# Attention, gated layer and hard-swish layer on one core: the seven-product blocks' matmuls taken in alternation with those of the neighbouring products

## The chip, the core and the metric

The kernel runs on one core of a Trainium2 chip. The metric is the device time of one execution in microseconds, the median of several. The engines are TensorE (PE, with its weight loads PEld), VectorE (DVE), ScalarE (ACT), GpSimd (POOL, which here mostly issues DMAs) and SyncE (SP, which issues the loads from memory). Each engine takes its instructions in the order in which the program has them.

## The reference

Three layers follow each other. `x` of the second is the first's output, 896 tokens of 768 numbers.

```python
attn = softmax(causal(scale * q @ k.T)); x = attn @ v             # 2 x 12 heads, 448 tokens, 64 wide
gate = 1.0 / (1.0 + np.exp(-(x @ w_gate))); val = x @ w_val       # 768 -> 1536, twice
x = (gate * val) @ w_out                                          # 1536 -> 768
h = x @ w_in; g = h * np.clip(h + 3.0, 0.0, 6.0) / 6.0            # 768 -> 2048
out = g @ w_out2                                                  # 2048 -> 768
```

## The kernel before

**Numbers.** The weights come as 64-bit words. Each unit of 128 x 768 is loaded by SP and made into float32 by five steps (`dec_scale` on ACT, line 115; `dec_shift`, `dec_clamp`, `dec_join`, `dec_sign` on DVE, lines 120, 124, 128, 134). Every operand of a matmul is then split into a rounded part `hi` and a rest `lo`, and every product of two operands is three matmuls (`TERMS`: hi with hi, hi with lo, lo with hi). A split is done in one of two ways. `split` (lines 181 and 182) and `dec_hi`/`dec_lo` (153 and 158) copy on ACT and subtract on DVE. `dma_split` (142 to 144) copies and negates on ACT and lets a DMA issued by POOL add the source onto the negative: in the rows that DMA is `lo<-S` or `lo<-raw`.

**Stages.** Attention goes first. The gate and value layer follows with eight plain units (`halves`, line 190) and then the FIRST run of seven-product blocks. `halves` again makes the 1536 -> 768 product and then four plain units of the 2048-wide layer. The THIRD run of seven-product blocks does the rest of that layer, and `block` (line 1203) the last product. In `halves` each set of weights is used twice in a row, for two halves of the tokens, which go to two PSUM banks: its matmuls alternate between banks already. `block` and the seven-product blocks keep to one bank for a whole product.

**Seven-product blocks.** `Pairs.run` takes two weight units at a time (a pair p; eight pairs in FIRST, six in THIRD). The four quarters of the two units and of the activations are combined by sums (`w_sums`, DVE lines 727 to 730), so that seven half-sized products P1 to P7 do the work of eight. A product (`product`, line 750) is nine matmuls of 128 x 448: three chunks of the inner dimension times three terms. A pair has three PSUM banks. Bank 0 collects P1, then P6, then P7, then P4; what stands there between two of them is copied out by ACT (`copy_out`, line 767) before the next may add to it. Bank 1 collects P5 and then P3 and is added by DVE (`add_out`, line 771); bank 2 holds P2. The order on PE is P1(p), P2(p), P4(p-1), P6(p), P3(p-1), P5(p), P7(p); after the last pair come its P4 and P3. The weights of a product are named by their group: group 1 for P1 and P2 (`g`), group 2 for P6 and P5 (`hi`, `lo`), group 3 for P7 and P3 (`hi`, `lo`), group 4 for P4 (`g`). Groups 2 and 3 of the next pair are made by `dma_split` from the sums, one pair ahead. `finish` and `p4_out` apply the gate (`glu`, ACT line 919 and DVE line 917) or the hard swish (`hardswish`, ACT 1087 and DVE 1088), and `end1`, `end2`, `end3` start the splits that the next stage needs.

Of the kernel before, what the change touches and what calls it, by code (L numbers as in the profile page):

```python
# [21 lines left out]
TERMS = ((0, 0), (0, 1), (1, 0))  # L22
# [9 lines left out]
def kernel(  # L32
# [12 lines left out]
    nc = tc.nc  # L45
# [4 lines left out]
    P = 128  # L50
# [14 lines left out]
    HK = KD // 2  # L65
# [145 lines left out]
    with tc.manual_schedule():  # L211

        with ExitStack() as actx:
# [212 lines left out]
            def product(cols, stationary=P):  # L426

                return max(cols / 2.4 + 3, stationary / 1.2)


            steps = []
            for p in range(NP):
# [11 lines left out]
                for i, ts in enumerate(STILES):  # L444
                    work = sum(
                        6 * product(Q1[t], Q1[t] - Q0[t]) + 2 * product(Q1[t] - Q0[t], 0) for t in ts
                    )
                    add(f"S{i}", "pe", work, ["Tlq", "Tlk"], s_pe, ts)
                    for t in ts:
                        add(f"M{t}", "dve", 70 + 2.1 * Q1[t], [f"S{i}"], s_max, t)  # L450
                for t in range(NQ):
                    n = Q1[t]
# [3 lines left out]
                for g in range(NG):  # L456
                    m = WIDTH[g]
                    tiles = [f"N{t}" for t in range(NQ) if Q1[t] > GROUPS[g][0][0] * D]
                    add(f"C{g}", "pe", 0.87 * m, tiles, c_pe, g)
                    add(f"H{g}", "act", 60 + m / 1.2, [f"C{g}"], c_hi, g)  # L460
                    add(f"J{g}", "dve", 70 + m / 0.96, [f"H{g}"], c_lo, g)
                    work = sum(3 * product(S - c * D) for c, _ in GROUPS[g])
                    add(f"D{g}", "pe", work, [f"J{g}", "Vl", f"D{g - 1}"][: 2 + (g > 0)], d_pe, g)
# [13 lines left out]
            for u in range(3):  # L477
                w = f"{u}"
# [188 lines left out]
        def w_dec():  # L667

            i = stream[0]
            stream[0] += 1  # L670
            u = order[i]
            decode_a(u)
            if i + 3 < NU:
                load_unit(order[i + 3])
            if u not in in_pairs:
                behind.append(u)

        def w_parts():
            while behind:
                u = behind.pop(0)  # L680
                (dec_dma if u < len(order1) else decode_b)(u)

        def tiles_at(i, n):
            return [gact.tile([P, UN], F32R, tag=f"e{i + x}", name="g") for x in range(n)]

        class Pairs:
# [7 lines left out]
            def __init__(self, units, form, s_at, g1_at, g4_at, hold, p4_out, finish, ahead):  # L694
                self.units, self.form, self.hold = units, form, hold
                self.s_at, self.g1_at, self.g4_at = s_at, g1_at, g4_at
                self.P4_out, self.finish, self.ahead = p4_out, finish, ahead
                self.n = len(units)
                self.grp, self.banks = {}, {}

            def w_g1(self, p):
                if p < self.n:
# [40 lines left out]
                self.w_g(p, 3)  # L743

            def product(self, ps, w, off, nm, first):
                x = self.form[nm]
                for i in range(HK):
                    k = off * HK + i
                    for n, (a, c) in enumerate(TERMS):
                        nc.tensor.matmul(  # L750
                            ps,
                            lhsT=w[a][:, k * P : (k + 1) * P],
                            rhs=x[:, c, i],
                            start=(first and i == 0 and n == 0),
                            stop=(i == HK - 1 and n == 2),
                            skip_group_check=True,
                        )

            def P1(self, p):
                self.banks[p] = [  # L760
# [45 lines left out]
            def P3_add(self, p):  # L806
                self.add_out(p, 1, "C12")

            def run(self, end1, end2, end3):

                for p in range(self.n):
                    end = p == self.n - 1
                    self.P1(p)
                    self.P1_out(p)
                    if p:
                        self.P7_add(p - 1)
                    if p or not self.ahead:  # L820
                        self.w_g1(p + 1)
                        w_dec()
                    self.P2(p)
                    self.w_g1_lo(p + 1)
                    self.P2_add(p)
                    if p:
                        self.P4(p - 1)
                        self.P4_out(p - 1)
                    self.P6(p)
                    self.P6_out(p)  # L830
                    if self.ahead and p == 0:
                        y_split("T4")
                    self.w_sums(p + 1)
                    if p:
                        self.P3(p - 1)
                        self.P3_add(p - 1)
                    if end:
                        end1()
                    self.w_g4(p + 1)
                    self.w_g2(p + 1)  # L840
                    self.P5(p)
                    soon = p and self.soon(p - 1)
                    if not end:
                        w_parts()
                    if soon:
                        self.finish(p - 1)
                    if not end:
                        w_dec()
                    if p and not soon:
                        self.finish(p - 1)  # L850
                    self.P7(p)
                    self.P7_out(p)
                    if end:
                        self.P7_add(p)
                        end2()
                    else:
                        self.w_g3(p + 1)
                p = self.n - 1
                self.P4(p)
                self.P4_out(p)  # L860
                self.P3(p)
                w_parts()
                end3()
                self.P3_add(p)
                self.finish(p)
# [64 lines left out]
        def g4_at1(p):  # L930
            return [t[:, :HU] for t in tiles_at(4 * (p % 2) + 2, 2)]

        first = Pairs(
            [(at1[f, v], at1[f + 1, v]) for f, v in pairs1], form1, s1_at,
            lambda p: tiles_at(4 * (p % 2), 2), g4_at1, hold1, p4_out1, finish1, False,
        )
# [127 lines left out]
        def y_split(nm):  # L1064
            form3[nm] = gact.tile([P, 2, HK, S], F32R, tag=f"r{nm}", name=nm)
            h, b = {"T2": (0, 0), "T1": (0, 1), "T4": (HK, 0), "T3": (HK, 1)}[nm]
            for i in range(HK):
                split(
                    form3[nm][:, 0, i], form3[nm][:, 1, i], yr[h + i][:, b * S : (b + 1) * S]
                )  # L1070
# [199 lines left out]
```

## Time and profile before

| | us |
|---|---|
| median of 3 runs (606.36 to 607.29) | 607.05 |
| span of the profiled execution | 604.3 |
| PE busy in it | 591.4 |
| DVE busy | 476.4 |
| ACT busy | 346.1 |
| the chain that ended last, by engine | PE 56%, DVE 27%, ACT 9%, POOL 3%, DMA 2% |

The profile covers one execution from its first to its last instruction; what its own time has beside the span is not recorded, and the median of the runs lies 2.75 us above the span. A matmul's row in the trace lasts about 365 ns and overlaps the next one; the distance between the starts of two matmuls is what one costs. An "idle" in brackets is time in which no row of that engine runs, with the name of what ended it, so a wait is somewhat longer than the idle beside it.

### The profile page before, as it was taken

Reading aid. Unit: us, or ns where it says so; the run is one execution under the profiler, and the core shown is the slowest. Engines: PE = TensorE matmul, PEld = TensorE weight load, DVE = VectorE, ACT = ScalarE, POOL = GpSimd, SP = SyncE. Lnnn points to the kernel's source line nnn. Section 1 sums busy time; section 2 is a strip of 40 time slices with the busy share of each in tenths; the row PEclk is TensorE's granted clock in tenths of the full one; section 3 lists DMA queues with packets and bytes.
Section 4 is the critical chain, followed back from the end, with each engine's and each line's share of the span. In section 5 each row is a group of like instructions: output and inputs, shape, how many; then the busy total and the mean of one; then the engine's idle time right before and its main releaser. Section 6 shows DMA issues by size and latency. Waiting matters only on the chain.

```text
span 604.3 us, 9071 instructions
## 1 busy us (share of the span) xinstructions
PE 591.4 (98%) x3372; PEld 535.8 (89%) x3372; DVE 476.4 (79%) x739; ACT 346.1 (57%) x680; POOL 136.7 (23%) x195
## 2 busy tenths in 40 slices
PE   8999999999999999999999999999999999999997
PEld 4788788899998999998999999988999899999997
DVE  6789998568797898988967787888999888867601
ACT  3898998735656656667443333387677645533200
POOL 4889988401111111110000000012222000000000
PEclk9999999999999999999999999999999999999999
DMA  7665341036985876674334434367988514437002
GB/s 167 137 178 132 81 143 33 0 79 167 263 178 133 215 183 180 166 177 129 82 114 150 154 115 135 94 165 165 235 217 200 140 53 112 131 124 227 23 1 91
DMA packets 86684, 82.64 MB, mean 137 GB/s; under 512 B 35312, under 2 KB 77040, under 8 KB 86640
## 3 DMA queue, kind: packets, MB, share of 16 engines
q1 hardware_dynamic: 80448, 64.50, 35.9%
q0 software_dynamic: 6192, 17.57, 15.8%
q8 instruction: 26, 0.43, 0.3%
q14 instruction: 18, 0.15, 0.1%
HBM read 61.73 MB, written 2.75 MB: 107 GB/s over the span
## 4 chain that ended last, share of the span: by engine, by line
PE 56%; DVE 27%; ACT 9%; POOL 3%; issue 3%; DMA 2%; SPq 0%; ACTq 0%; POOLq 0%; DVEq 0%
PE w L750 25%; PE m L1203 12%; PE m L190 10%; DVE b L128 4%; DVE b L134 4%; DVE lo L158 4%; PE pav L392 3%; ACT hi L153 3%; PE s L309 2%; DVE g L1171 2%; PE pt L365 2%; DVE b L124 2%; DVE raw L120 2%; ACT pr L337 2%; DVE g L182 2%
## 5 line engine op out<-in xcount | busy, mean ns | idle before, releaser
L1203 PE MATMUL m<-hi,g 128*128 128x384 f32 x448 | 114.0, 335 | 0.6 <-DVE g L1171 0.6
L153 ACT CAST hi<-b 128x768 fp32r<-128x768 f32 x35 | 29.0, 835 | 104.3 <-DVE b L134 100.1
L1203 PEld LDWEIGHTS m<-hi,g 128*128 128x128 f32 x448 | 80.8, 188 | 1.2 <-DVE g L1171 1.2
L1203 PE MATMUL m<-lo,g 128*128 128x384 f32 x224 | 74.9, 335 | 0.4 <-DVE lo L158 0.4
L750 PE MATMUL w<-T,hi 128*128 128x448 f32 x252 | 72.4, 368 | 1.4 <-ACT g2r L767 1.4
L190 PE MATMUL m<-g,hi 128*128 128x448 f32 x288 | 70.1, 365 | 0.0
L134 DVE SCALAR_TENSOR_TENSOR b<-raw,b 128x768 int32<-128x768 int32 x68 | 66.0, 971 | 2.3
L128 DVE SCALAR_TENSOR_TENSOR b<-b,raw 128x768 int32<-128x768 int32 x68 | 65.4, 962 | 2.3
L115 ACT ACTIVATE b<-raw 128x768 f32<-128x768 f32 x68 | 61.2, 905 | 0.0
L124 DVE TENSOR_SCALAR b<-b 128x768 f32<-128x768 f32 x68 | 38.1, 561 | 25.5 <-ACT b L115 25.2
L190 PEld LDWEIGHTS m<-g,hi 128*128 128x128 f32 x288 | 54.1, 188 | 4.3
L144 POOL DMA_DIRECT2D lo<-S x26 | 25.2, 971 | 131.0 <-ACT lo L143 102.5
L352 POOL TENSOR_SCALAR pr<-pr,rc 64x64 f32<-64x64 f32 (+3 forms) x96 | 52.6, 565 | 9.1 <-DVE rc L346 7.3
L158 DVE TENSOR_TENSOR lo<-b,hi 128x768 fp32r<-128x768 f32 x35 | 33.3, 957 | 27.0 <-ACT hi L153 26.9
L750 PEld LDWEIGHTS w<-T,hi 128*128 128x128 f32 x252 | 47.2, 188 | 6.3 <-ACT g2r L767 1.8
L190 PE MATMUL m<-x,hi 128*128 128x448 f32 x192 | 49.1, 367 | 0.0
L337 ACT ACTIVATE pr<-s,nm 64x64 f32<-64x64 f32 (+3 forms) x96 | 44.4, 469 | 5.7 <-PE s L319 5.0
L750 PE MATMUL w<-T,lo 128*128 128x448 f32 x126 | 46.5, 369 | 0.7 <-DMA lo<-S 0.5
L1203 PEld LDWEIGHTS m<-lo,g 128*128 128x128 f32 x224 | 42.0, 188 | 0.7 <-DVE lo L158 0.7
L392 PE MATMUL pav<-pth,vpad 128*128 128x448 f32 (+6 forms) x168 | 41.0, 309 | 0.0
L190 PE MATMUL m<-g,lo 128*128 128x448 f32 x144 | 40.9, 366 | 0.0
L190 PEld LDWEIGHTS m<-x,hi 128*128 128x128 f32 x192 | 35.7, 188 | 2.7
(139 smaller groups left out, 1248.8 us busy)
## 6 DMA issues: line engine op xcount, KB each, us to landing
raw<-in_moe_w_out_dram SPq DMA_DIRECT2D x28, 768.0 KB, 4.5
raw<-in_moe_w_in_dram SPq DMA_DIRECT2D x16, 768.0 KB, 4.7
lo<-S POOLq DMA_DIRECT2D x26, 384.0 KB, 4.3
raw<-in_moe_w_gate_dram SPq DMA_DIRECT2D x12, 768.0 KB, 5.2
raw<-in_moe_w_val_dram SPq DMA_DIRECT2D x12, 768.0 KB, 5.0
k<-in_k_dram SPq DMA_DIRECT2D x24, 112.0 KB, 2.7
q<-in_q_dram SPq DMA_DIRECT2D x24, 112.0 KB, 3.0
v<-in_v_dram SPq DMA_DIRECT2D x24, 112.0 KB, 2.9
```

Source lines behind the costliest of these rows:

```text
L115: nc.scalar.activation(b, words(u)[0].bitcast(F32), AF.Copy, scale=REBIAS)
L124: nc.vector.tensor_scalar(b, b, UPPER_MAX, -UPPER_MAX, op0=ALU.min, op1=ALU.max)
L128: nc.vector.scalar_tensor_tensor(bi, bi, 3, words(u)[1], op0=ALU.logical_shift_left, op1=ALU.bitwise_or)
L134: nc.vector.scalar_tensor_tensor(bi, words(u)[0], -(2 ** 31), bi, op0=ALU.bitwise_and, op1=ALU.bitwise_or)
L153: nc.scalar.copy(hi, part_t[u])
L158: nc.vector.tensor_sub(lo, part_t.pop(u), split_t[u][0].bitcast(F32))
L190: nc.tensor.matmul(ps[:, b, :S], lhsT=w[a][:, i * P : (i + 1) * P], rhs=x(c, k0 + i, b), start=(first and i == 0 and n == 0), stop=(last a ...
L337: nc.scalar.activation(pr[:, :, j], ps[:, j].rearrange("p (c d) -> p c d", d=D), AF.Exp, bias=nm[:, j : j + 1], accum_out=sm[:, j : j + 1],)
L352: nc.gpsimd.tensor_scalar(pr[:, :, j], pr[:, :, j], rc[:, j : j + 1], 1.0, op0=ALU.mult, op1=ALU.mult)
L392: nc.tensor.matmul(live["pav", p][:, c * D :], lhsT=vpad[p % NV][a][:, c], rhs=pt[e][:, off : off + S - c * D], start=(c == 0 and m == 0), ...
L750: nc.tensor.matmul(ps, lhsT=w[a][:, k * P : (k + 1) * P], rhs=x[:, c, i], start=(first and i == 0 and n == 0), stop=(i == HK - 1 and n == ...
L1203: nc.tensor.matmul(po[t], lhsT=g2[2 * s + i][a][:, t * P : (t + 1) * P], rhs=w[e][:, i * HC : (i + 1) * HC], start=(s == 0 and i == 0 and ...
```

## The change

`product` no longer emits its nine matmuls in one piece. It emits the first four in alternation with the five that the product before it left over, and leaves its own last five to the next call. `flush` emits what is left where no product follows at once. The readers of a product stand one product later in the program, since a product now ends in its successor's call. In the last pair P3 comes before P4, and what bank 1 holds of P5 is copied out by ACT (`P5_out`) before P3 adds to it, while bank 0 with P7 is added by DVE (`P5_add`) before P4. `P7_out` and `w_g3` move from the end of a pair to the start of the next.

```diff
             def product(self, ps, w, off, nm, first):
                 x = self.form[nm]
-                for i in range(HK):
+                def one(i, n, a, c):
                     k = off * HK + i
-                    for n, (a, c) in enumerate(TERMS):
-                        nc.tensor.matmul(
...
+                steps = [(i, n, a, c) for i in range(HK) for n, (a, c) in enumerate(TERMS)]
+                head = len(steps) // 2
+                for m in range(max(len(self.rest), head)):
+                    if m < len(self.rest):
+                        self.rest[m]()
+                    if m < head:
+                        one(*steps[m])
+                self.rest = [lambda st=st: one(*st) for st in steps[head:]]
+
+            def flush(self):
+                for mm in self.rest:
+                    mm()
+                self.rest = []
...
+            def P5_out(self, p):
+                nc.scalar.copy(self.hold(p, "C22"), self.banks[p][1])
+
+            def P5_add(self, p):
+                self.add_out(p, 0, "C22")
...
                     self.P1(p)
+                    if p:
+                        self.P7_out(p - 1)
+                        self.w_g3(p)
+                    self.P2(p)
                     self.P1_out(p)
                     if p:
                         self.P7_add(p - 1)
                     if p or not self.ahead:
                         self.w_g1(p + 1)
                         w_dec()
-                    self.P2(p)
+                    if p:
+                        self.P4(p - 1)
+                    else:
+                        self.flush()
                     self.w_g1_lo(p + 1)
                     self.P2_add(p)
+                    self.P6(p)
                     if p:
-                        self.P4(p - 1)
                         self.P4_out(p - 1)
-                    self.P6(p)
+                        self.P3(p - 1)
+                    else:
+                        self.flush()
                     self.P6_out(p)
...
+                    self.P5(p)
                     if p:
-                        self.P3(p - 1)
                         self.P3_add(p - 1)
...
-                    self.P5(p)
+                    self.P7(p)
+                    if end:
+                        self.P5_out(p)
...
-                    self.P7(p)
-                    self.P7_out(p)
-                    if end:
-                        self.P7_add(p)
-                        end2()
-                    else:
-                        self.w_g3(p + 1)
                 p = self.n - 1
+                self.P3(p)
+                self.P5_add(p)
+                end2()
                 self.P4(p)
+                self.flush()
                 self.P4_out(p)
-                self.P3(p)
                 w_parts()
                 end3()
                 self.P3_add(p)
```

On PE at the start of the FIRST run, before (`x_70` is P1's operand, `x_72` P2's, `T_2308` P6's, the rows above are the plain units):

```order
L190 MATMUL m<-x_72,lo 128x448
L190 MATMUL m<-x_73,lo 128x448
L750 MATMUL w<-x_70,g 128x448 x9
L750 MATMUL w<-x_72,g 128x448 x9
L750 MATMUL w<-T_2308,hi 128x448 x2
```

and now:

```order
L751 MATMUL w<-x_70,g 128x448 x5
L751 MATMUL w<-x_72,g 128x448
L751 MATMUL w<-x_70,g 128x448
L751 MATMUL w<-x_72,g 128x448
L751 MATMUL w<-x_70,g 128x448
L751 MATMUL w<-x_72,g 128x448
L751 MATMUL w<-x_70,g 128x448
L751 MATMUL w<-x_72,g 128x448
L751 MATMUL w<-x_70,g 128x448
L751 MATMUL w<-x_72,g 128x448 x5
L751 MATMUL w<-T_2308,hi 128x448 x2
```

P1 ended with PE's ninth matmul of the run and now ends with its thirteenth; P6 starts with the nineteenth in both.

On PE at the end of the THIRD run, before (`T_4492` is P7's operand, `T_4594` P4's, `y_3667` P3's; line 1203 is the next stage):

```order
L750 MATMUL w<-T_4492,hi 128x448 x2
L750 MATMUL w<-T_4492,lo 128x448
L750 MATMUL w<-T_4594,g 128x448 x9
L750 MATMUL w<-y_3667,hi 128x448 x2
```

and now:

```order
L751 MATMUL w<-T_4492,hi 128x448
L751 MATMUL w<-y_3667,lo 128x448
L751 MATMUL w<-T_4492,hi 128x448
L751 MATMUL w<-y_3667,hi 128x448
L751 MATMUL w<-T_4492,lo 128x448
L751 MATMUL w<-y_3667,hi 128x448
L751 MATMUL w<-T_4594,g 128x448
L751 MATMUL w<-y_3667,lo 128x448
L751 MATMUL w<-T_4594,g 128x448
L751 MATMUL w<-y_3667,hi 128x448
L751 MATMUL w<-T_4594,g 128x448
```

P4, which stood between P7 and P3, is now the last product, and five of its matmuls follow P3's end.

On ACT in the last pair of the THIRD run, before (`h<-g2r` and `t<-g2r` are `finish` of the pair before, the copy between the two `g` rows is the one of bank 0 after P7):

```order
L767 COPY g2r<-w 128x448
L1170 ACTIVATE g_5191<-g2r 128x896
L1087 ACTIVATE h<-g2r 128x448
L1087 ACTIVATE t<-g2r 128x896
L767 COPY g2r<-w 128x448
L1170 ACTIVATE g_5191<-g2r 128x896
L1087 ACTIVATE h<-w 128x448
L153 CAST hi<-b 128x768 x2
```

and now, with the new copy of bank 1 after P5:

```order
L782 COPY g2r<-w 128x448
L1198 ACTIVATE g_5195<-g2r 128x896
L825 COPY g2r<-w 128x448
L1115 ACTIVATE h<-g2r 128x448
L1115 ACTIVATE t<-g2r 128x896
L1198 ACTIVATE g_5195<-g2r 128x896
L1115 ACTIVATE h<-w 128x448
L153 CAST hi<-b 128x768 x2
```

The copy moved ahead of `finish`; the same happens at the end of FIRST. Apart from this move, ACT, DVE, POOL and SP have the same instructions in the same order as before, in both runs.

## Rows read from the trace of the kernel before

**Rows 1.** The page: span, busy time of the engines, and one line of its DMA issues.

```profile
span 604.3 us, 9071 instructions
...
PE 591.4 (98%) x3372; PEld 535.8 (89%) x3372; DVE 476.4 (79%) x739; ACT 346.1 (57%) x680; POOL 136.7 (23%) x195
...
lo<-S POOLq DMA_DIRECT2D x26, 384.0 KB, 4.3
```

**Rows 2.** Busy time by stretch, FIRST and line 190's: engines, granted clock, DMA.

```profile
179.20:284.30 105.10, 104.30 (x505) 94.45 (x504) 91.62 (x141) 66.29 (x100) 13.32 (x14) 1.00 0.67 173
284.30:401.10 116.80, 116.80 (x577) 108.12 (x577) 94.59 (x131) 51.03 (x71) 2.80 (x4) 1.00 0.41 119
```

**Rows 3.** Timeline, PE in FIRST: start of P1 of pairs 0 to 3.

```profile
179.21 3.81 PE L750 MATMUL w<-x,g 128*128 128x448 f32 x18
...
188.32 3.81 PE L750 MATMUL w<-x,g 128*128 128x448 f32 x18
...
201.67 3.88 PE L750 MATMUL w<-x,g 128*128 128x448 f32 x18
...
214.69 1.61 PE L750 MATMUL w<-x,g 128*128 128x448 f32 x7
```

**Rows 4.** Timeline, start of FIRST: ACT's first copy and split, PE's P6(1).

```profile
181.23 0.53 ACT L767 COPY raw<-w 128x448 f32<-128x448 f32 x1 [4.96 <-PE w L750]
...
188.37 0.83 ACT L142 CAST hi<-raw 128x768 fp32r<-128x768 f32 x1 [1.91 <-DVE raw L728]
...
194.54 0.47 PE L750 MATMUL w<-T,lo 128*128 128x448 f32 x1 [0.18 <-DMA lo<-raw]
```

**Rows 5.** Timeline, group 2's DMA in FIRST and THIRD; the PE row is P6(7)'s.

```profile
201.96 1.20 POOL L144 DMA_DIRECT2D lo<-S  x1 [8.15 <-PE w L750]
...
267.69 0.84 POOL L144 DMA_DIRECT2D lo<-S  x1 [8.29 <-ACT lo L143]
...
272.76 0.37 PE L750 MATMUL w<-T,lo 128*128 128x448 f32 x1
...
426.29 1.20 POOL L144 DMA_DIRECT2D lo<-S  x1 [5.94 <-ACT lo L143]
...
465.35 1.19 POOL L144 DMA_DIRECT2D lo<-S  x1 [5.93 <-ACT lo L143]
```

**Rows 6.** Timeline, end of FIRST: P7's last matmul, P4, DVE, line 190.

```profile
279.58 0.37 PE L750 MATMUL w<-T,lo 128*128 128x448 f32 x1
280.57 2.09 PE L750 MATMUL w<-T,g 128*128 128x448 f32 x9 [0.62 <-ACT h L767]
...
285.14 0.56 PE L190 MATMUL m<-g,lo 128*128 128x448 f32 x2
...
280.55 0.62 DVE L771 TENSOR_TENSOR h<-w,h 128x448 f32<-128x448 f32 x1 [1.66 <-ACT h L767]
...
283.94 1.82 DVE L158 TENSOR_TENSOR lo<-b,hi 128x768 fp32r<-128x768 f32 x2
```

**Rows 7.** Timeline, PE at the start of THIRD: P6(0) and P6(1).

```profile
406.33 0.67 PE L750 MATMUL w<-T,hi 128*128 128x448 f32 x2 [1.39 <-ACT g2r L767]
...
418.46 0.47 PE L750 MATMUL w<-T,lo 128*128 128x448 f32 x1 [0.52 <-DMA lo<-S]
```

**Rows 8.** Timeline, end of THIRD: PE, ACT and DVE.

```profile
478.45 2.09 PE L750 MATMUL w<-T,g 128*128 128x448 f32 x9 [0.62 <-ACT g2r L767]
...
482.89 0.44 PE L1203 MATMUL m<-lo,g 128*128 128x384 f32 x1 [0.35 <-DVE lo L158]
...
475.07 0.95 ACT L1087 ACTIVATE t<-g2r 128x896 f32<-128x896 f32 x1
...
480.58 0.55 ACT L1087 ACTIVATE h<-w 128x448 f32<-128x448 f32 x1 [1.33 <-PE w L750]
...
476.49 1.08 DVE L1088 SCALAR_TENSOR_TENSOR g2r<-t,g2r 128x896 f32<-128x896 f32 x1
...
481.88 1.83 DVE L158 TENSOR_TENSOR lo<-b,hi 128x768 fp32r<-128x768 f32 x2
```

More of the change, by code (lines that the diff above doesn't have):

```diff
@@ L698, in __init__ @@
                 self.n = len(units)
-                self.grp, self.banks = {}, {}
+                self.grp, self.banks, self.rest = {}, {}, []
             def w_g1(self, p):
@@ L746, in product @@
                 x = self.form[nm]
-                for i in range(HK):
+                def one(i, n, a, c):
                     k = off * HK + i
-                    for n, (a, c) in enumerate(TERMS):
-                        nc.tensor.matmul(
[L751 to L757, printed above, removed]
+                    nc.tensor.matmul(
+                        ps,
+                        lhsT=w[a][:, k * P : (k + 1) * P],
+                        rhs=x[:, c, i],
+                        start=(first and i == 0 and n == 0),
+                        stop=(i == HK - 1 and n == 2),
+                        skip_group_check=True,
+                    )
+                steps = [(i, n, a, c) for i in range(HK) for n, (a, c) in enumerate(TERMS)]
[10 more added lines that the diff above has]
+                self.rest = []
             def P1(self, p):
```

## The prediction

> **What bounds the kernel now.** The page comes first: PE is busy 591.4 us of a span of 604.3 [rows 1], so the kernel ends when PE has got through its matmuls, and time can be won only from the pace of a matmul or from PE's few waits. The table by stretch shows the TensorE clock at its upper level (1.00 of 2.4 GHz) in FIRST as in the stage of line 190 [rows 2].
>
> The pace is read from starts. FIRST begins with P1, P2, P6, P5, P7 of pair 0, 45 matmuls, from 179.21 to P1(1) at 188.32: 202.4 ns each. From P1(2) at 201.67 to P1(3) at 214.69 lie 63 in 13.02 us: 206.7 ns [rows 3]. Line 190, which alternates between two banks, makes 577 in 116.80 us, 202.4 ns [rows 2]. So there are two paces 4.3 ns apart, and one bank alone has both; the slower one begins behind P6(1)'s wait for `lo`.
>
> The waits of the two runs stand in three kinds of places. P6(1) waits for the DMA that makes its `lo` [rows 4, 7]. P6(0) of THIRD waits for ACT [rows 7]. In the last pair P4 waits until ACT has copied P7 out of bank 0: 279.58 to 280.57 is 0.99 where 0.20 is usual [rows 6], and THIRD shows the same idle of 0.62 [rows 8]. Line 1203 then waits for its first `lo` [rows 8].
>
> Beside PE runs a chain that it does not pace: sums on DVE, `hi` and the negative on ACT, POOL's DMA, the next decode, `w_g1`, the next sums. Group 2's DMA goes out at 201.96 and five pairs later at 267.69, 13.15 us a pair; in THIRD at 426.29 and three pairs later at 465.35, 13.02 [rows 5]. That is as long as PE's own 13.02, so a faster PE would soon wait for it. Its slack at P6(7): issue 267.69, landing 4.3 later by the page's median [rows 1] = 272.0, use 272.76 [rows 5].
>
> **The change, part by part.** Let a position be one matmul (0.207 us). A product's first four matmuls now stand 4, 3, 2 and 1 positions earlier, its last one 4 later; only the third needs `lo`, 2 positions (0.41) earlier. The number of matmuls stays the same, and no DMA is moved past another.
>
> *In the middle pairs: 0.* A copy-out that waits for PE comes 0.83 later, and bank 0 still has ten positions between two products. No row there shows DVE or the chain of group 2 waiting behind those copies for long. The cover is the chain's slack of about 0.8 against 0.41 asked. Without it each pair would lose up to 0.4.
>
> *(a) Start of FIRST: +1.2.* P1(0) ends 4 positions later (0.81 at 202.4 ns). ACT has been idle 4.96 us for it [rows 4], and behind that copy stand `w_g1`, the decode scale, through it DVE's decode and sums, and ACT's `hi<-raw`, which waited for DVE [rows 4]. All of it comes 0.81 later, and so does the `lo` for which P6(1) waits at 194.54 [rows 4]. This `lo` is now needed two positions earlier in the row, so PE has 0.41 more behind it: 0.81 + 0.41 = 1.22.
>
> *(b) Last pair of FIRST: +0.6.* Before, one wait: 0.99 - 0.20 = 0.79, and one slow step after it (0.1: the row at 194.54 [rows 4], also behind a wait, lasts 0.47 where those of [rows 5, 6] last 0.37), 0.9 in all. Now two. P3's first matmul stands two positions behind P5's last and waits for the copy: 0.99 - 0.41 + 0.1 = 0.68. P4's first stands two behind P7's last and waits for DVE's add, 0.62 [rows 6] where the copy takes 0.53 [rows 4]: 0.77. Together 1.45, so 0.55 more.
>
> *(c) Into line 190: +1.0.* P4 is now last. DVE's multiply of its result (0.62, the form of the add in [rows 6]) and then the first of two subtractions for the next stage's `lo` (1.82 for both [rows 6], 0.91 each) follow P4's end; before, P3's nine matmuls covered them and 285.14 shows no idle [rows 6]. From P4's last start: 0.37 + 0.04 + 0.6 + 0.95 = 1.95; line 190 uses `lo` five positions (1.0) later, so 0.95, and 0.1 after it.
>
> From here to THIRD the same chain of DVE and ACT is late by (a) to (c), and P6(0) of THIRD waits for ACT anyhow, 1.39 idle [rows 7]; nothing is lost again.
>
> *(d) Start of THIRD: +0.4.* The chain there does not hang on P1(0)'s end, since ACT comes late to it. The `lo` at 418.46 [rows 7] comes as before and finds PE two positions further from the end: 0.41.
>
> *(e) Last pair of THIRD: +0.95.* First wait 0.68 as in (b). With (d) P5's last matmul starts at 477.46 (0.99 before P4 [rows 8]) + 0.41 - 5 x 0.207 = 476.83. The copy is done at 476.83 + 0.41 + 0.53 = 477.77, P3 starts at 477.82, P7's last at 477.82 + 0.10 + 7 x 0.2025 = 479.34. Behind that copy on ACT now stand `finish`'s two steps, the second of which was done at 475.07 + 0.95 = 476.0 before [rows 8]; ACT's `t` (0.95) ends at about 479.1, DVE's step with it takes 1.08 [rows 8], and only then comes the add of 0.62: 480.8. P4's first would have been at 479.75, so 1.05 and 0.1 after it. 0.68 + 1.15 - 0.88 = 0.95.
>
> *(f) Into line 1203: +1.8.* Before, P4 ended at 480.54 (ACT starts on it at 480.58 [rows 8]) and line 1203's first `lo` matmul ran at 482.89, behind ACT's relu, ACT's `hi` and DVE's `lo` at 481.88 [rows 8]: 2.35. With P4 last that is 2.35 + 0.37 after its last start, where 0.41 is usual: 2.3 lost, and 0.1. Before, 0.6 was lost there. So 1.8.
>
> *(g) Pace: between 0 and -1.0, taken -0.3.* If the pairs keep the 206.7 ns that followed a wait for `lo` in [rows 3], nothing changes. If they keep 202.4, each pair is 0.27 us shorter until PE meets the chain of 13.15 and 13.02. Banks leave less: P6 now starts four positions earlier behind ACT's copy. I allow 0.55 in FIRST and 0.45 in THIRD. Line 190's alternation speaks for the fast pace, the wait for `lo` that remains against it, so a third of it is taken.
>
> Sum: 1.2 + 0.55 + 1.05 + 0.4 + 0.95 + 1.8 - 0.3 = 5.65. On the span 604.3 that gives about 609.9; with the 2.75 us by which the median of the runs lies above it, 612.7.
>
> The Trainium skill, "TensorE: Matmul & The Clock Gate", section "Back-to-back issue gap", gives an isolated warm gap of N / 2.4 + 2.5 ns whatever the bank, which would be 189 ns for 448 columns. The trace disagrees with 202.4 and 206.7; by the page neither bank nor order would change the pace, and (g) would be 0.
>
> **The rivals.**
> *The ends cost less.* The `lo` subtractions may be got through earlier, or the next stage may make up the delay in slack that I did not see, so that (c) and (f) are nothing: 612.7 - 2.85 = 609.9. For it speaks that line 1203 has only 0.6 of wait there now; against it that DVE and ACT take their instructions in order and both stand behind P4's result.
>
> *Line 190's stage falls to the slow pace* after its new wait: 577 x 4.3 ns = 2.5 us, of which 1.5 vanish in P6(0)'s wait [rows 7]: 613.7, up to 615.2 if that cover is gone. No row shows the slow pace in alternating matmuls.
>
> *Faster: alternating lifts the pace itself* for all 882 matmuls of the blocks (14 pairs of 7 products of 9). Losses of 5.95 are repaid when a matmul costs 6.7 ns less than the mean of about 205.8, that is below 199 ns, and only if the chain of group 2 is not what holds the pairs. At 189 ns (the distance that pure streaming at 2.4 GHz would nearly give, 448 / 2.4 = 187) it would be 613.0 - 882 x 16.8 ns = 598.2. Against it: line 190 alternates and has 202.4 [rows 2], and the chain's 13.15 us a pair is longer than 63 x 202.4 = 12.75. The gap of 189 ns that the Trainium skill gives on the page named above is the same number.
>
> *No change:* the copy of P1(0) or the waits of the last pairs are covered by something that I misread, and the fast pace gives back the rest: 607.
>
> *The clock falls.* At 1.2 GHz 448 columns take 373 ns, and 882 x 167 ns = 147 us. Line 190 alternates at 1.00 [rows 2]. The Trainium skill, "TensorE: Matmul & The Clock Gate", section "A second HAM failure mode: psum-queue depth-cycling", tells of a kernel that lost clock by cycling banks in every iteration; by that rule this change would be dangerous, by the row it is not.
>
> **How the numbers follow.** The forecast, (a) to (g) as summed, 611.8 to 613.3: 0.52. Ends cheaper, 609.3 to 611.8: 0.20. Slower pace in line 190 or a further wait in the middle pairs, 613.3 to 615.5: 0.14. No change, within 0.2% (1.2 us, about what runs of this kernel can tell apart): 0.06. Faster pace: 0.06. Clock: 0.02. The range 609.4 to 614.5 leaves out the last three and the far end of the third case. Faster 0.06, same 0.06, slower 0.88.
>
> **What would show it.** In FIRST P6(1)'s `lo` matmul starts near 195.35, with a longer idle before it. Each last pair shows two idles before PE rows, one ended by ACT's copy, one by DVE's add, the second longer in THIRD. The first `lo` of line 190 shows a wait for DVE's subtraction, that of line 1203 one of about 2 us. Group 2's DMAs stay 13.15 and 13.02 apart. The prediction is wrong if the distance between starts in the pairs drops below 199 ns, if those DMAs draw closer together, or if the ends of the runs show no longer waits.

## The result and the profile after

The changed kernel takes 612.33 us (median of 6 runs, 611.62 to 613.56) against 606.7 of the kernel before (6 runs, 604.41 to 608.58). The ratio is 1.0105, 95% interval 1.0085 to 1.0124: slower by 6.4 us (5.2 to 7.5); the two medians lie 5.6 apart. The forecast was 612.7, from 609.4 to 614.5.

The page of the profiled execution, its first line and the one of busy times [rows 1]:

```profile
span 610.6 us, 9072 instructions
...
PE 595.1 (97%) x3372; PEld 536.1 (88%) x3372; DVE 476.3 (78%) x739; ACT 345.7 (57%) x680; POOL 136.3 (22%) x195
```

The number of matmuls is the same and the span is 6.3 us longer. By stretch (FIRST, line 190's, and 3.2 us at the start of the last product; the columns as in [rows 2]):

```profile
179.10:285.60 106.50, 104.06 (x505) 93.96 (x504) 90.67 (x139) 66.53 (x101) 13.29 (x14) 1.00 0.66 171
285.60:405.66 120.06, 119.30 (x577) 108.03 (x576) 96.57 (x133) 52.54 (x74) 3.50 (x5) 1.00 0.40 117
...
490.40:493.60 3.20, 3.20 (x12) 3.20 (x12) 2.72 (x4) 3.20 (x4) 0.00 (x0) 0.51 0.00 0
```

FIRST is 1.4 us longer than before and line 190's stage 3.3. The third row is a surprise that is taken up at the end: the clock granted there is half.

The start of FIRST, ACT's copy of P1(0) and PE's P6(1), in the timeline [rows 4]:

```profile
181.94 0.54 ACT L782 COPY raw<-w 128x448 f32<-128x448 f32 x1 [5.76 <-PE w L751]
...
195.23 0.47 PE L751 MATMUL w<-T,lo 128*128 128x448 f32 x1 [0.33 <-DMA lo<-raw]
```

FIRST begins at 179.11, 0.10 earlier than before. ACT has been idle 5.76 us where it was 4.96, and `lo` is used 16.12 us behind the start where it was 15.33.

The end of FIRST, PE and then DVE (L825 is the new copy of bank 1, L786 the add, L945 the multiply of P4's result) [rows 6]:

```profile
280.12 0.48 PE L751 MATMUL w<-x,hi 128*128 128x448 f32 x1 [0.42 <-ACT h L825]
...
282.81 0.47 PE L751 MATMUL w<-T,g 128*128 128x448 f32 x1 [0.58 <-DVE h L786]
...
285.60 0.99 PE L190 MATMUL m<-g,hi 128*128 128x448 f32 x4
287.35 0.68 PE L190 MATMUL m<-g,lo 128*128 128x448 f32 x2 [0.76 <-DVE lo L158]
...
282.13 0.62 DVE L786 TENSOR_TENSOR h<-w,h 128x448 f32<-128x448 f32 x1 [1.79 <-PE w L751]
...
285.80 0.62 DVE L945 TENSOR_TENSOR raw<-w,raw 128x448 f32<-128x448 f32 x1 [1.05 <-PE w L751]
286.34 1.82 DVE L158 TENSOR_TENSOR lo<-b,hi 128x768 fp32r<-128x768 f32 x2
```

There are three waits where there was one: P3 for ACT's copy, P4 for DVE's add, and line 190 for a `lo` that DVE begins only at 286.34, behind the multiply of P4's result. Before, that subtraction ran at 283.94, under P3's matmuls.

In the middle pairs of FIRST PE has waits that are not in the trace of before. P4 of pair 0 idles 0.70 us for ACT's copy of P7 (at 191.93, hidden there, since P6(1) has to wait for `lo` behind it), P4 of pair 3 loses 0.2 us, and P4 of pair 5 waits until ACT has done two gate steps (L947) and then the copy. PE, then ACT:

```profile
257.46 0.47 PE L751 MATMUL w<-T,g 128*128 128x448 f32 x1 [0.39 <-ACT h L782]
...
255.59 1.41 ACT L947 ACTIVATE raw<-raw 128x448 f32<-128x448 f32 x2
256.90 0.51 ACT L782 COPY h<-w 128x448 f32<-128x448 f32 x1
```

Group 2's DMA, first and last of those compared [rows 5], and the start of THIRD [rows 7]:

```profile
202.65 1.20 POOL L144 DMA_DIRECT2D lo<-S  x1 [8.14 <-ACT lo L143]
...
268.31 0.84 POOL L144 DMA_DIRECT2D lo<-S  x1 [8.27 <-ACT lo L143]
...
429.26 1.20 POOL L144 DMA_DIRECT2D lo<-S  x1 [5.94 <-ACT lo L143]
...
468.34 1.19 POOL L144 DMA_DIRECT2D lo<-S  x1 [5.94 <-ACT lo L143]
```

```profile
405.66 2.64 PE L751 MATMUL w<-y,g 128*128 128x448 f32 x12
...
421.46 0.47 PE L751 MATMUL w<-T,lo 128*128 128x448 f32 x1 [0.35 <-DMA lo<-S]
```

The DMAs stand 65.66 / 5 = 13.13 and 39.08 / 3 = 13.03 us apart, as before. THIRD starts 4.5 us later than before, but its P6(1) only 3.0: P6(0)'s wait for ACT (1.76 from one matmul to the next, 1.55 above the usual) is gone, since PE is now later than ACT there.

The end of THIRD, PE, ACT and DVE (L1115, L1116 are the hard swish, L1231 the last product) [rows 8]:

```profile
480.51 0.47 PE L751 MATMUL w<-y,hi 128*128 128x448 f32 x1 [0.42 <-ACT g2r L825]
...
483.50 0.47 PE L751 MATMUL w<-T,g 128*128 128x448 f32 x1 [0.86 <-DVE g2r L786]
...
487.80 0.45 PE L1231 MATMUL m<-hi,g 128*128 128x384 f32 x1 [1.35 <-ACT hi L153]
488.79 0.44 PE L1231 MATMUL m<-lo,g 128*128 128x384 f32 x1 [0.55 <-DVE lo L158]
...
486.48 0.54 ACT L1115 ACTIVATE h<-w 128x448 f32<-128x448 f32 x1 [3.86 <-PE w L751]
486.92 1.56 ACT L153 CAST hi<-b 128x768 fp32r<-128x768 f32 x2
...
481.81 1.09 DVE L1116 SCALAR_TENSOR_TENSOR g2r<-t,g2r 128x896 f32<-128x896 f32 x1 [0.22 <-ACT t L1115]
482.82 0.62 DVE L786 TENSOR_TENSOR g2r<-w,g2r 128x448 f32<-128x448 f32 x1
...
487.06 0.62 DVE L1116 SCALAR_TENSOR_TENSOR g2r<-h,w 128x448 f32<-128x448 f32 x1 [2.62 <-ACT h L1115]
487.77 1.83 DVE L158 TENSOR_TENSOR lo<-b,hi 128x768 fp32r<-128x768 f32 x2
```

The add ahead of P4 is held up by DVE's step with `t`, as the prediction had it, and ACT, idle for 3.86 us, must take the relu of P4's result before it may begin the next stage's `hi`.

### The profile page after: what moved, and what is told of

It is laid out like the page before. It is cut to its first block, busy times and chain, and to the rows that moved or that the text cites. A ratio compares the mean times of both kernels' runs of the same rounds, so it can differ in the third digit from the quotient of the medians.

```text
span 610.6 us, 9072 instructions
## 1 busy us (share of the span) xinstructions
PE 595.1 (97%) x3372; PEld 536.1 (88%) x3372; DVE 476.3 (78%) x739; ACT 345.7 (57%) x680; POOL 136.3 (22%) x195
## 3 DMA queue, kind: packets, MB, share of 16 engines
HBM read 61.73 MB, written 2.75 MB: 106 GB/s over the span
## 4 chain that ended last, share of the span: by engine, by line
PE 78%; DVE 10%; ACT 5%; POOL 2%; issue 2%; DMA 1%; SPq 0%; ACTq 0%; POOLq 0%; DVEq 0%
PE m L190 29%; PE m L1231 19%; PE w L751 16%; PE pav L392 5%; PE s L309 4%; PE pt L365 3%; DVE b L128 1%; ACT b L115 1%; PE s L319 1%; PE tr L277 1%; POOL pr L352 1%; DVE g L712 1%; DVE vpad L592 1%; DVE b L124 1%; POOL vpad L271 1%
## 5 line engine op out<-in xcount | busy, mean ns | idle before, releaser
L1231 PE MATMUL m<-hi,g 128*128 128x384 f32 x448 | 115.1, 337 | 1.4 <-ACT hi L153 1.4
L751 PE MATMUL w<-T,hi 128*128 128x448 f32 x252 | 84.1, 367 | 0.0
L1231 PEld LDWEIGHTS m<-hi,g 128*128 128x128 f32 x448 | 81.8, 190 | 1.7 <-ACT hi L153 1.7
L1231 PE MATMUL m<-lo,g 128*128 128x384 f32 x224 | 75.5, 337 | 0.5 <-DVE lo L158 0.5
L751 PE MATMUL w<-T,g 128*128 128x448 f32 x126 | 45.7, 373 | 2.7 <-DVE g2r L786 0.9
L1231 PEld LDWEIGHTS m<-lo,g 128*128 128x128 f32 x224 | 42.6, 190 | 0.8 <-DVE lo L158 0.8
```

The source lines that it names most:

```text
L751: nc.tensor.matmul(ps, lhsT=w[a][:, k * P : (k + 1) * P], rhs=x[:, c, i], start=(first and i == 0 and n == 0), stop=(i == HK - 1 and n == ...
L1231: nc.tensor.matmul(po[t], lhsT=g2[2 * s + i][a][:, t * P : (t + 1) * P], rhs=w[e][:, i * HC : (i + 1) * HC], start=(s == 0 and i == 0 and ...
```

## The experiments

What comes ahead of FIRST differs by up to 2.3 us between executions of one program (the kernel before starts FIRST at 179.21 in one trace and at 181.43 in another, the changed one at 179.11 and 181.45). The difference goes with the clock: in the fourteen traces FIRST starts at 179.1 to 179.2 where no stretch ahead of it ran at half clock, at 180.5 to 180.7 where one did, and at 181.4 to 181.5 where two did (last section). So beside the timed ratio the table has a figure of the trace that leaves this out: from the start of FIRST's first matmul to the start of the kernel's last one.

| kernel | median, us | ratio to before (95%) | FIRST's first to last matmul, us |
|---|---|---|---|
| before | 605.9 to 606.8 | 1 | 421.05; again 420.75 |
| changed | 612.33 | 1.0105 (1.0085 to 1.0124) | 427.51; again 426.93 |
| e1 next stage's splits ahead of P4_out | 610.77 | 1.0072 (1.0049 to 1.0095) | 423.95 |
| e2 P1(0) whole | 611.2 | 1.0086 (1.0064 to 1.0108) | 425.44 |
| e3 last pair as before | 608.39 | 1.0032 (1.0015 to 1.0049) | 421.76 |
| e4, e10 whole products, last pair swapped | 604.53; 604.11 | 0.9972 (0.9954 to 0.9990); 0.9969 (0.9952 to 0.9985) | 418.30; 418.19 |
| e5 alternation in the middle alone | 608.21 | 1.0018 (1.0004 to 1.0033) | 421.01 |
| e6 as e4, splits behind P4_out | 607.63 | 1.0023 (1.0008 to 1.0039) | 422.38 |
| e7, e11 middle alternates, ends of e4 | 605.24; 605.25 | 0.9976 (0.9961 to 0.9991); 0.9989 (0.9976 to 1.0001) | 419.26; 419.47 |
| e12 as e7, P7's copy ahead of finish | 611.49 | 1.0083 (1.0062 to 1.0104) | 424.56 |

**e1, the order on DVE and ACT.**

```diff
-                self.P4_out(p)
                 w_parts()
                 end3()
+                self.P4_out(p)
```

> The changed kernel, but in the last pairs the steps that start the next stage's splits (w_parts and end3) stand ahead of P4_out. Theory (DVE and ACT take their steps in order, so the next stage's first hi and lo stand behind P4's result): line 190's first wait for DVE's lo (1.03 us more than before) and line 1203's two waits for ACT's hi and DVE's lo (1.8 us more) go, and with them the stretch at the lower clock in line 1203: 612.3 - 2.8 = 609.5, or less if the clock stays up. Part of line 190's 1.0 may be taken back in P6(0)'s wait of the THIRD run. Rival (the next stage's start is late because its inputs are late, whatever stands ahead of it on DVE): the waits stay and the time is 611.5 or more.

Measured: 610.77, by the ratios 2.0 us less than the changed kernel, where 2.8 or more was expected (the two intervals just overlap), by the trace 3.0 to 3.6 less. PE at the starts of line 190's stage and of the last product:

```profile
286.93 0.97 PE L190 MATMUL m<-g,hi 128*128 128x448 f32 x4
287.74 0.57 PE L190 MATMUL m<-g,lo 128*128 128x448 f32 x2
...
486.57 0.34 PE L1231 MATMUL m<-hi,g 128*128 128x384 f32 x1
486.75 0.33 PE L1231 MATMUL m<-lo,g 128*128 128x384 f32 x1
```

All three waits are gone, and so is the stretch at half clock; P6(0)'s wait of 1.5 us is back in THIRD and takes its part of the gain. So it was the place behind P4's result that made the next stage late, and not its inputs.

**e2, the start of FIRST.** P1 of pair 0 is flushed before P2:

```diff
                         self.w_g3(p)
+                    else:
+                        self.flush()
                     self.P2(p)
```

> The changed kernel, but P1 of pair 0 is taken whole, so that it ends with the run's ninth matmul as before. Theory (the chain of sums hangs on P1(0)'s end in the FIRST run): P6(1)'s lo matmul there comes 0.8 us earlier, near 194.5, and the kernel takes 612.3 - 0.8 = 611.5, or down to 611.1. Rival (the chain starts elsewhere, or the gain is lost again in waits of the middle pairs or of P6(0) in the THIRD run): 612.3.

Measured: 1.2 us less by the ratios (1.0105 to 1.0086; the intervals overlap). FIRST begins at 180.63 in this trace; ACT and PE:

```profile
182.65 0.53 ACT L782 COPY raw<-w 128x448 f32<-128x448 f32 x1 [4.95 <-PE w L751]
...
195.96 0.47 PE L751 MATMUL w<-T,lo 128*128 128x448 f32 x1 [0.31 <-DMA lo<-raw]
```

`lo` is used 15.33 us behind the start, exactly as before, where the changed kernel had 16.12. The chain of sums hangs on P1(0)'s end.

**e3, the last pair as before.** Alternation stays in all other places:

```diff
...
                 p = self.n - 1
+                self.P7(p)
+                self.flush()
+                self.P7_out(p)
+                self.P7_add(p)
+                end2()
+                self.P4(p)
+                self.flush()
+                self.P4_out(p)
                 self.P3(p)
-                self.P5_add(p)
-                end2()
-                self.P4(p)
                 self.flush()
-                self.P4_out(p)
```

> The changed kernel with alternation in all pairs, but at the end of a run P7, P4 and P3 are whole and in the old order, with the old copies. Theory (the loss is mostly at the ends of the two runs): the terms of the last pairs and of the next stages' starts go (0.66 + 1.03 + 0.94 + 1.8 measured in the trace), 612.3 - 4.4 = 607.9; what stays is the start of both runs, less the pace. Rival (alternation in the middle pairs costs by itself): 610 or more.

Measured: 608.39, by the ratios 4.4 us less than the changed kernel (0.0073 x 606). Two thirds of the loss sit at the ends of the two runs.

**e4, whole products in the new order.** The kernel before with P3 ahead of P4 in the last pair, and the next stage's splits ahead of P4_out:

```diff
                     self.P7(p)
-                    self.P7_out(p)
                     if end:
-                        self.P7_add(p)
-                        end2()
+                        nc.scalar.copy(self.hold(p, "C22"), self.banks[p][1])
...
-                self.P4(p)
-                self.P4_out(p)
                 self.P3(p)
+                self.add_out(p, 0, "C22")
+                end2()
+                self.P4(p)
                 w_parts()
                 end3()
+                self.P4_out(p)
```

> The kernel before with whole products, and at the end of a run only the order changed: P3 ahead of P4 (bank 1 copied out by ACT after P5, bank 0 added by DVE after P3), and w_parts and end3 ahead of P4_out. Theory (it is alternation that puts a bank's reader and its next writer two matmuls apart, not P3 ahead of P4): nine whole matmuls now cover each copy, so the wait of 0.9 us in each last pair goes and so does the 0.6 ahead of line 1203: 606.7 - 2.4 = 604.3; with line 190's part taken back in P6(0)'s wait of the THIRD run, 605.2. Rival (P3 ahead of P4 costs, since P4's result is what the next stage waits for): 608 or more.

Measured: faster than before, 0.9972, and 0.9969 when run once more. The end of FIRST, ACT, DVE and PE (L853 is the copy of bank 1, L771 the add):

```profile
279.78 0.52 ACT L853 COPY h<-w 128x448 f32<-128x448 f32 x1
...
281.37 0.63 DVE L771 TENSOR_TENSOR h<-w,h 128x448 f32<-128x448 f32 x1 [0.48 <-PE w L750]
...
282.92 1.98 PE L750 MATMUL w<-T,g 128*128 128x448 f32 x9
284.74 0.98 PE L190 MATMUL m<-g,hi 128*128 128x448 f32 x4
```

The copy and the add lie under nine matmuls of the other bank each, and no row of PE there has an idle. So P3 ahead of P4, with the next stage's splits ahead of P4's result, is the better end; e1 has the same order with alternated products, and keeps the waits of the last pairs (0.42 and 0.58 us idle in FIRST, 0.42 and 0.88 in THIRD). What cost there was to alternate.

**e6, which half of e4 does it.** As e4, with the order on DVE and ACT of the changed kernel:

```diff
+                self.P4_out(p)
                 w_parts()
                 end3()
-                self.P4_out(p)
```

> The kernel before with whole products and P3 ahead of P4 at the end of a run, but w_parts and end3 stand behind P4_out as in the changed kernel. Theory (the next stage waits because DVE and ACT take the multiply of P4's result first, whether products alternate or not): line 190's first lo waits about 1.0 us and line 1203's first hi and lo 2.4, while the last pairs lose nothing: 604.5 + 1.0 + 2.4 = 607.9, or 607.3 where the THIRD run's P6(0) takes some of it back. Rival (alternation made these waits): 604.5.

Measured: 607.63, 3.1 us above e4 by the ratios. PE:

```profile
284.21 0.68 PE L190 MATMUL m<-g,lo 128*128 128x448 f32 x2 [0.77 <-DVE lo L158]
...
482.74 0.44 PE L1204 MATMUL m<-hi,g 128*128 128x384 f32 x1 [1.35 <-ACT hi L153]
483.74 0.44 PE L1204 MATMUL m<-lo,g 128*128 128x384 f32 x1 [0.56 <-DVE lo L158]
```

These are the changed kernel's waits to 0.01 us, with whole products. The waits at the starts of the next stages belong to the order (P4 last, its result first on DVE and ACT), those in the last pairs to alternation.

**e5 and e7, the middle pairs.** e5 has the edits of e2 and e3 together; e7 has e2's start, alternation in the middle and e4's ends:

```diff
...
                 p = self.n - 1
+                self.P7(p)
+                self.flush()
+                self.P5_out(p)
                 self.P3(p)
+                self.flush()
                 self.P5_add(p)
                 end2()
                 self.P4(p)
                 self.flush()
-                self.P4_out(p)
                 w_parts()
                 end3()
+                self.P4_out(p)
```

> The changed kernel with alternation in the middle pairs alone: P1 of pair 0 whole, and the end of a run as before (P7, P4 and P3 whole, in the old order). Theory (all of the loss is at the starts and ends of the two runs): the kernel before with the 0.4 us that the lo of the THIRD run's P6(1) costs when it is used two matmuls earlier, and with between 0 and 1.0 us of pace: 606.0 + 0.4 - 0.5 = 605.9, from 605.4 to 606.5. Rival (alternation also costs in the middle pairs, where P4 waits for ACT's copy by up to 0.5 us three times): 607.5 or more.

> Alternation in the middle pairs alone, P1 of pair 0 whole, and the end of a run with whole products, P3 ahead of P4 and the next stage's splits ahead of P4_out: the best of both. Theory (alternation in the middle is worth nothing either way): as with whole products everywhere, 604.5, within 0.6. Rival 1 (the middle gains by the pace): 603.5. Rival 2 (the waits for ACT's copy in the middle cost): 605.5.

Measured: e5 608.21, 1.1 us above before by its ratio (0.2 to 2.0), while its trace is as long as those of before. By the time the rival stood nearer, by the trace the theory. The granted clock that is on record for every execution decides for the rival. At 0.999 or 1.000, which in the traces goes with no stretch at half clock ahead of FIRST, e5's four executions take 606.2 to 606.7 and the twelve of before that were timed beside them 604.4 to 605.9 (middle 605.1): 1.4 us more; at 0.993 to 0.994 it is 1.2. The traces of before hide this, because they are not typical of it: the first has a span of 604.3, and all 32 timed executions of before at that clock have 602.6 to 604.2. So alternation in the middle pairs costs some 1.3 us. The `lo` of P6(1), used two matmuls earlier in both runs, makes 0.8 of it (the theory had counted only THIRD's), and P4 of pair 3 another 0.4 (below).

e7 is as fast as e4 within the intervals, with 1.0 us more in the trace. Two kernels were run side by side:

> Whole products with P3 ahead of P4 at the end of a run and the next stage's splits ahead of P4_out, once more, to stand beside the same ends with alternation in the middle on one chip. Theory (with PE at 202.7 ns alternation leaves the copy of P7 less time and costs 0.8 us in FIRST): 604.5, some 0.8 less than the next kernel. Rival (no difference): the same time within 0.4.

> Alternation in the middle pairs alone, with the same starts and ends as the kernel above. Theory: 605.3, 0.8 above it, with waits of 0.2 and 0.5 us for ACT's copy ahead of P4 in FIRST. Rival: 604.5.

604.11 against 605.25, and 418.19 against 419.47 in the traces. FIRST alone takes 103.26 and 103.27 with whole products, 104.10 and 104.13 with alternation: 0.85 in each pair of traces. Of it 0.41 is the `lo` of P6(1) that is used two matmuls earlier, and the rest is at P4 of pair 3, which ACT's copy of P7 lets in 0.2 us late (e7 at 230.49, e11 at 230.47), with two slow steps after it. The intervals of the ratios overlap, but the four traces agree, and so do the times at one granted clock: at 0.999 or 1.000 the middle ones are 603.4 and 604.6, at 0.993 to 0.994 605.6 and 606.4.

**e12, ACT's order.** As e7, but `finish` of a pair stands behind the copy of the next pair's P7:

```diff
                         self.P7_out(p - 1)
+                        if p > 1:
+                            self.finish(p - 2)
                         self.w_g3(p)
...
-                    if soon:
+                    if end and soon:
                         self.finish(p - 1)
...
-                    if p and not soon:
+                    if end and p and not soon:
                         self.finish(p - 1)
```

> As the kernel above, but on ACT the copy of P7 stands ahead of finish of the pair before, so that it no longer waits for the two gate steps of 1.4 us. Theory A (it is ACT's order that makes P4 wait): the waits ahead of P4 of 0.2 and 0.5 us in FIRST go and nothing takes their place: 604.6, 0.7 less. Theory B (PE at 202.7 ns has caught up with the chain of sums of 13.15 us a pair, and P4 is only where it shows): the waits move to P6 or to the lo of the next group, and the time stays at 605.3. More than 606: finish, now later, holds up the decode or the next stage.

Measured: 611.49, the case of more than 606 on record. The first of three waits of this size in FIRST, PE and ACT:

```profile
220.98 0.47 PE L751 MATMUL w<-T,hi 128*128 128x448 f32 x1 [1.24 <-ACT h L782]
...
220.39 0.53 ACT L782 COPY h<-w 128x448 f32<-128x448 f32 x1 [2.30 <-DVE raw L954]
```

In the middle pairs of FIRST P4 waits no more, but P6 does: ACT's copy of P1 into `h` stands still for 2.30 us until DVE's gate step of the delayed `finish` is through. The wait moved to P6, as theory B said, but to a cause that `finish` itself made, and it became larger than the one removed.

**e8 and e9, the same programs again.**

> The changed kernel once more, for its trace. Theory (behind each of its waits PE takes up one of two distances, 202.6 or 206.7 ns, and keeps it to the next wait; which one is not decided by the program): some stretches show the other distance than in the first trace, as line 190's stage, at 206.7 there, did in the variants. With 202.6 in it THIRD starts 0.8 us earlier (2.3 less, of which P6(0)'s wait takes back 1.5). The 3 us at 1.2 GHz at the start of line 1203 may be missing too, 1.4 us less. Rival (the program decides): the same distances and the same fall of the clock, span 610.6.

> The kernel before once more, for its trace. Theory (the distance between matmuls is taken up anew behind each wait and is not decided by the program): FIRST, 206.7 ns behind P6(1)'s wait in the first trace, may show 202.7 here, and then PE comes up to 1.6 us closer to the end of FIRST, less what it waits for the chain of sums. If so, the middle pairs of whole products can run as fast as alternating ones, and the first trace of before was one of its slower executions there. Rival (whole products run at 206.7 and alternating ones at 202.7): 206.7 again.

e8: behind the same wait for `lo`, line 190 goes on at 202.8 ns for 70 matmuls and at 206.7 after a pause of 0.1 us; in the first trace it had 206.7 all through. A stretch of 115 matmuls in the middle of FIRST has 206.6 where it had 202.7. Line 1231 waits as long, and the clock does not fall. THIRD starts 0.2 us earlier against FIRST's start, not 0.8. e9: FIRST has 206.7 again, which fits the rival; but line 190 has 206.7 where it had 202.7, and THIRD 202.7 where it had 206.6. Line 190's stage of the kernel before, a stretch of 78 us in the first trace and in the second (busy times of that line alone):

```profile
302.00:380.00 78.00, 78.00 (x386) 72.30 (x386) 1.00 0.42 132
```

```profile
304.00:382.00 78.00, 78.00 (x380) 70.84 (x379) 1.00 0.42 132
```

The program and the clock are the same, and 386 or 380 matmuls begin. So one trace's distance is no property of the code in these stages. In FIRST before has 206.7 in both its traces, e4 and e10 have 202.7 in both, and e6 a mean of 204.2 up to P4 of pair 5, though the instructions of these kernels are the same there up to the last pair. So the instructions of the stage do not fix the distance there either; what does stays open.

## Why the prediction was right

The terms, counted in the two first traces (distances between matmuls above the usual one, and the slow step behind each wait):

| term | predicted | measured | from |
|---|---|---|---|
| (a) start of FIRST | +1.2 | +1.20 | 16.12 - 15.33, and two matmuls more behind `lo` (0.41) |
| (b) last pair of FIRST | +0.55 | +0.66 | 0.58 + 0.75 beyond the usual distance, and 0.1 twice, against 0.88 |
| (c) into line 190 | +1.05 | +1.03 | the `lo` row, e1 and e6 |
| (d) start of THIRD | +0.4 | +0.41 | P6(1)'s `lo` is matmul 73, before 75 |
| (e) last pair of THIRD | +0.95 | +0.94 | 1.82 of waits against 0.88 |
| (f) into the last product | +1.8 | +1.82 | 2.44 against 0.62 |
| (g) pace, and middle pairs (0) | -0.3 | -0.83 | FIRST -0.52, THIRD -0.31 |
| line 190's pace | rival | +0.8 | 2.3 slower, 1.55 given back in P6(0)'s wait |
| last product | none | +0.45 | 1.6 of clock, 1.1 of later waits that went |
| sum | 5.65 | 6.5 | spans: 6.3, starts of FIRST: 0.1 |

**The ends** went as forecast, each wait at its place, behind the engine named. e1, e2, e3 and e6 take them away or bring them alone, at their prices. The rival by which the ends cost less is refuted.

**The pace and the middle pairs** were mis-sized. The sum has -0.3 for both together, from a third of the allowance of 0.55 and 0.45 and a 0 for the middle pairs; the first traces give -0.83. From P6(1)'s `lo` in FIRST to the matmul ahead of the last pair's first wait there are 409 distances in 84.10 us, before 411 in 85.04: 205.6 against 206.9 ns. That is two parts. Most stretches ran at 202.7 ns instead of 206.7, which is worth 1.6 us, and 1.1 us of it went in the new waits of the middle pairs and the slow steps behind them, which the prediction had put at nothing. What remains, 0.52, is close to the allowance, but PE was not held up where the prediction looked: neither at group 2's DMA, which kept its 13.13 us a pair, nor at P6, but at P4, by ACT's copy of P7. The wait at P4 of pair 5 comes with the faster pace (e4 has it too, 0.34 us idle), the one at P4 of pair 3 with alternation. That alternation made the faster pace is not shown: whole products had it in FIRST as well (e4, e10).

Against before as it usually runs, pace and middle pairs gained nothing: e5, which has these and the two `lo` (0.8), is 1.2 to 1.4 us slower at one granted clock, and with the ends of e4 for both, e11 is some 1 us slower than e10. The break-even of 199 ns was never near.

**Line 190 at the slow pace**, a rival with its share in 0.14, came true in the first trace, at the price it was given (2.3 - 1.55 where 2.5 - 1.5 stood). The argument against it, that no alternating matmuls had shown that pace, was weak: line 190's matmuls alternate in both traces of before, and have 202.7 in one and 206.7 in the other (e9).

**The time.** The sum of 5.65 lies in the interval of the ratio (5.2 to 7.5) and beside the 5.6 between the medians; before measured 606.7 in these runs instead of 607.05, and by this much the forecast is high. (Every timed execution on record takes 1.7 to 1.8 us more than its span; the other 0.9 of the 2.75 that the forecast added is the distance of one traced execution from the median of three.) Of the first traces' 6.5, 1.25 are the last two rows ahead of the sum, which were not in the forecast and differ between executions; 0.5 of (g) is what it took back. e8 against e9 gives 426.93 - 420.75 = 6.2. At granted clocks of 0.999 or 1.000 the changed kernel's three executions take 611.6 to 612.3 (middle 611.7) and before's 32 have 605.1 in the middle. They were not timed side by side, so the 6.6 between them is an estimate; the six terms of starts and ends make 6.06 of it. Starts and ends carried the forecast; that the whole came within 0.4 us of the median is partly luck, since pace, middle pairs, line 190 and the last product together cost some 0.5 where the sum had -0.3.

**Clock by alternation**, the rival after the Trainium skill's "TensorE: Matmul & The Clock Gate", section "A second HAM failure mode: psum-queue depth-cycling": the windows show 1.00 through FIRST with two or three banks in turn, so this kernel does not show that failure.

## What to carry to other kernels

Alternating two accumulations does not add matmuls, but it ends the first later and begins the second's successor earlier: count the matmuls between a bank's last write and its next first one, and compare them with the copy and with all that stands ahead of it on its engine. At the end of a run put first what the next stage needs, on the engines that make its operands too; here the swapped order with whole products gained 1.7 to 1.9 us while the same order with alternated products lost 2.4 (e1 against e3). Before a term is read from a distance between matmuls, look at a second trace of the same program. Compare times of executions with the same granted clock, and see where the traced execution stands among the timed ones.

## What the runs showed of the hardware

**Two distances, 202.7 and 206.7 ns.** At a granted clock of 1.00 PE takes up one of the two behind a wait, also one of 0.1 us, and mostly keeps it until the next (in the first traces 410 matmuls of FIRST before, 629 from line 190 into THIRD after). In between there are only stretches that seem to mix both (204.2 in e6). What chooses was not found; the program does not in line 190's stage and in THIRD (e8, e9), and in FIRST whole products had either (before, e4).

**Half clock behind a wait, in some executions.** At the start of the last product the changed kernel's PE started two matmuls in 2.7 us (idle 1.35 and 0.55), and from 490.4 to 493.6 ten matmuls stood 320 ns apart where 174 is usual, at a granted clock of 0.51, the level of 1.2 GHz: 1.6 us lost. e6, with whole products and the same waits, shows it too:

```profile
484.46:487.66 3.20, 3.20 (x12) 3.20 (x12) 2.72 (x5) 2.54 (x4) 0.00 (x0) 0.50 0.00 0
```

e2 and e8 wait as long and stay at 1.00. So such a wait can cost another 1.6 us, but does not always. Behind the wait of 0.6 in the two traces of before it was not seen.

The same happens ahead of FIRST, in attention. PE idles 1.43 to 1.45 us there 75 to 76 us after the start, in all fourteen traces, and in eight of them a stretch of over 3 us at half clock follows. Before in e9, and in the first trace (the wait, then 3.2 us):

```profile
75.90 0.33 PE L365 MATMUL pt<-identf,pr 128*128 128x128 f32 x1 [1.44 <-POOL pr L352]
76.60:79.80 3.20, 3.20 (x19) 2.66 (x16) 2.13 (x5) 1.33 (x3) 1.31 (x4) 0.50 0.02 5
```

```profile
75.21 0.33 PE L365 MATMUL pt<-identf,pr 128*128 128x128 f32 x1 [1.45 <-POOL pr L352]
76.60:79.80 3.20, 3.20 (x37) 2.98 (x36) 3.02 (x7) 2.10 (x6) 1.90 (x5) 1.00 0.02 5
```

In these 3.2 us PE has 19 matmuls or 37; with such a stretch FIRST starts 1.3 to 1.5 us later. Five of the eight traces have another one 11 to 15 us after the start, and FIRST starts 0.7 to 0.9 us later still; in these five PE had idled 0.5 to 0.9 us at 9 to 11 us, in the others at most 0.3. Among the timed executions of before the middle one takes 605.1 us at 0.999 or 1.000 and 607.5 at 0.993 to 0.994. What decides between the two behind the same wait was not found.
